# Attention products in odd slots, between the two projections, instead of at the head of even slots

## The chip, the cores and the metric

The kernel runs on one core of one Trainium2 chip. Time is device time in microseconds, the median of several executions; less is better. The program issues instructions to five engines: TensorE (PE, matmuls, with its weight loads shown as PEld), VectorE (DVE), ScalarE (ACT), GpSimd (POOL) and SyncE (SP, which issues transfers). Each engine works through its own queue in the order in which the program put the instructions there, and waits at an instruction until what it depends on is done.

## The reference

Thresholded attention, followed by a two-layer block with a hard-swish in between. Shapes: 8 batches, 8 heads, sequence 576, head size 64; then 4608 tokens, model width 512, inner width 2048.

```
scores = scale * matmul(q, k^T)                       # scale = 1/sqrt(64)
thresh = max(scores, axis=-1) - tau
scores = where(scores >= thresh, scores, -1e9)
attn   = exp(scores - max(scores)); attn /= sum(attn) + 1e-9
x      = matmul(attn, v), heads side by side          # 4608 x 512
h      = x @ w_in                                     # first projection
g      = h * clip(h + 3, 0, 6) / 6
out    = g @ w_out                                    # second projection
```

## The kernel before, in words

**Slots.** The attention of a batch is cut into 18 slots; a slot is one tile of 128 query rows for two heads (576 scores each). Eight batches make 144 slots, held in `queue`. Nothing is scheduled automatically: the order in which the Python code runs is the order in each engine's queue. Slots 0 to 13 run in a loop of their own, two at a time; slots 14 to 143 run one by one in the second loop, and what is left over runs after it.

**Score burst.** At the end of an even slot n, `burst(n + 2)` (L219) writes the scores of slots n+2 and n+3 on TensorE, the even one's last part ahead of the odd one's last part.

**Banks.** PSUM, the memory that matmuls write, is one tile `ps` of 8 banks with 512 columns each. `score_col` gives the place of the scores. An even slot has columns 896 to 1471 and 2432 to 3007 (banks 1 and 2, and banks 4 and 5); an odd slot has 64 to 639 and 1600 to 2175 (banks 0 and 1, and banks 3 and 4). First projections use bank 6 (`HB`), in some slots 7 or 0; second projections use bank 7 (`OB`). The attention products use the first 256 columns of a bank that `bank` hands out: bank 6 up to slot 13, then banks 2 and 5 in turn, and after the loop 2, 5, 0, 3 in turn.

**Max, mask, exp.** `sm_max` (L233) is a pass on VectorE for each head that copies the scores out of PSUM and takes their maximum. In slot n it is called for slot n+1, at the slot's head. GpSimd makes a bias of it (L242), ScalarE masks (L247) and takes the exponential (L252), VectorE a reciprocal (L255), GpSimd the normalised probabilities `pn` (L260), and a DMA transposes them into `pT` or, for the remaining 64 rows of each head, `pR` (L271).

**Products.** `multiply(n)` issues what the table `products` holds for slot n: `av_main` or `av_rest`, each ten groups of matmuls of probabilities and v (L289), and gives back copies out of PSUM into `xT` or `xR` on VectorE (L297, L306). The last product of a chunk of 256 rows also appends its eight first-projection items to the list `todo1`.

**Projections.** At a slot's head one item is taken from `todo1`, before `multiply` runs. `mm1` is the first projection (matmuls in L312), `mm1_relu` runs on ScalarE in odd slots (L330) and on VectorE in even slots (L332), `mm1_gate` on VectorE (L345). When the last item of a chunk has run, its pieces of the second projection go to the list `todo2`. `second` takes two of them in odd slots from 21 (`N2`) on (matmuls in L312 as well); a finished tile of four pieces is copied out by VectorE in the next even slot (`mm2_out`, L364) and written by SP.

**Other work.** Even slots hold transposes of q and k on VectorE (L96, L110); q, k and v are loaded by transfers that GpSimd's queue issues, at the end of a slot.

**Order in a slot of the second loop** (from slot 21): max of slot n+1, reciprocal of n-1, item taken, products and their copies, first projection, relu, gate, copy-out of a finished tile, second projection (odd slots), exponentials, masks, transposes, normalising, burst (even slots), output writes, loads.

Of the kernel before, what the change touches and what calls it, by code (L numbers as in the profile page):

```python
# [20 lines left out]
def kernel(  # L21
# [41 lines left out]
    ps = ps_pool.tile([P, 8, 512], F32, name="ps")  # L63
# [12 lines left out]
    def at(when, n, job):  # L76
        when.setdefault(n, []).append(job)
# [75 lines left out]
    def warm_up(count):  # L153
        for _ in range(count):
            nc.tensor.transpose(ps[:, OB, P:2 * P], identf[:], identf[:])
# [12 lines left out]
    now = -1  # L168
    turn = 0

    def bank():
        nonlocal turn
        turn += 1
        if now < N1:
            return ps[:, HB, 0:256]
        return ps[:, (2, 5)[turn % 2] if now < len(queue) else (2, 5, 0, 3)[turn % 4], 0:256]

    class Slot:
        pass
# [3 lines left out]
    queue = []  # L183
# [41 lines left out]
    def sm_max(sl):  # L225
        sl.s = s_pool.tile([P, 2, S], F32, tag="s", name="s")
        sl.m = stat_pool.tile([P, 2], F32, tag="m", name="m")
        sl.bias = stat_pool.tile([P, 2], F32, tag="bias", name="bias")
        sl.rsum = stat_pool.tile([P, 2], F32, tag="rsum", name="rsum")
        sl.rinv = stat_pool.tile([P, 2], F32, tag="rinv", name="rinv")  # L230
        for i in range(2):
            c0 = score_col(sl.n, i)
            nc.vector.tensor_scalar(out=sl.s[:, i, :], in0=ps_flat[:, c0:c0 + S],  # L233
                                    scalar1=1.0, scalar2=None, op0=Alu.mult, op1=Alu.max,
                                    accum_out=sl.m[:, i:i + 1])
            if sl.n < 3:
                sm_bias(sl, slice(i, i + 1))
        if sl.n >= 3:
            sm_bias(sl)
# [5 lines left out]
    def sm_mask(sl, i):  # L245
        s = sl.s[:, i, :]
        nc.scalar.activation(out=s, in_=s, func=Act.Prelu, bias=sl.bias[:, i:i + 1], scale=scale,  # L247
                             alpha=REJECT)

    def sm_exp(sl, i):  # L250
        s = sl.s[:, i, :]
        nc.scalar.activation(out=s, in_=s, func=Act.Exp, accum_out=sl.rsum[:, i:i + 1])  # L252

    def sm_recip(sl):
        nc.vector.reciprocal(out=sl.rinv[:], in_=sl.rsum[:])  # L255
# [36 lines left out]
    def av_main(b, hp, chunk):  # L292
        if hp == chunk == 0:
            xT[b] = x_pool.tile([P, KI, 512], BF16, tag="xT", name="xT")
        pb = bank()
        av(pb, b, hp, pts[b, hp, chunk], slice(0, 256))
        return lambda: nc.vector.tensor_copy(out=xT[b][:, hp, 256 * chunk:256 * chunk + 256], in_=pb)  # L297

    def av_rest(b):
        pb = bank()  # L300
        for hp in range(NPAIR):
            av(pb[:, 64 * hp:64 * hp + 64], b, hp, ptr[b, hp % 2], slice(64 * (hp // 2), 64 * (hp // 2) + 64))
        if b % 2 == 0:
            xR[b // 2] = x_pool.tile([P, KI, P], BF16, tag="xR", name="xR")
        o0 = 64 * (b % 2)
        return lambda: nc.vector.tensor_copy(out=xR[b // 2][:, :, o0:o0 + 64],  # L306
                                             in_=pb.rearrange("p (a b) -> p a b", a=NPAIR))
# [6 lines left out]
    def mm1(item, hb=HB):  # L314
        b, ni, c0 = item
        if c0 is None:
            for ki in range(KI):
                half_columns(ps[:, hb, :], xR[b // 2][:, ki, :], w_in_sb[:, ki, ni * P:ni * P + 512],
                             start=(ki == 0), stop=(ki == KI - 1))
        else:  # L320
            for n in range(2):
                for ki in range(KI):
                    half_columns(ps[:, hb, n * 256:(n + 1) * 256], w_in_sb[:, ki, (ni + n) * P:(ni + n + 1) * P],
                                 xT[b][:, ki, c0:c0 + 256], start=(ki == 0), stop=(ki == KI - 1))
        return ps[:, hb, :]

    def mm1_relu(hps, on_act):
        r = r_pool.tile([P, 512], F32, tag="r", name="r")[:]
        if on_act:
            nc.scalar.activation(out=r, in_=hps, func=Act.Relu, bias=three[:])  # L330
        else:
            nc.vector.tensor_scalar(out=r, in0=hps, scalar1=3.0, scalar2=0.0, op0=Alu.add, op1=Alu.max)  # L332
        return r

    def mm1_gate(item, hps, r):
        b, ni, c0 = item
        if c0 is None:
            if ni % 8 == 0:
                odd[0] = go_pool.tile([P, 1024], BF16, name="go")
            out = odd[0][:, ni % 8 * P:ni % 8 * P + 512]  # L340
        else:
            c0 += (b % 2) * (S + 64)
            out = gbuf[:, ni:ni + 2, c0:c0 + 256]
            r, hps = (x.rearrange("p (n w) -> p n w", n=2) for x in (r, hps))
        nc.vector.scalar_tensor_tensor(out=out, in0=r, scalar=6.0, in1=hps, op0=Alu.min, op1=Alu.mult)  # L345
        if c0 is None and ni % 8 == 4:
            nc.sync.dma_start_transpose(out=gbuf[:, ni - 4:ni + 4, 512:512 + P], in_=odd[0][:])
# [33 lines left out]
    def whole(b, chunk):  # L381
        mt = 5 * (b % 2) + 2 * chunk
        items = [((b, ni, 256 * chunk), ()) for ni in range(0, NI, 2)]
        items[-1] = (items[-1][0], [(b // 2, mt + i, part) for i in range(2) for part in range(4)])
        return items

    def odd_items(b, halves):
        items = [((b, ni, None), ()) for half in halves for ni in (8 * half, 8 * half + 4)]
        if 1 in halves:
            items[-1] = (items[-1][0], [(b // 2, 4, part) for part in range(4)])  # L390
        return items

    products = {}
    for b in range(B):
        n0 = b * NSLOT
        for hp in range(NPAIR):
            at(products, n0 + (6 if b == 0 else 8) + 2 * hp, (b, hp, 0))
            at(products, n0 + 18 + 2 * hp, (b, hp, 1))
        at(products, n0 + (14 if b == 0 else 16), (b, None, None))

    def multiply(n):
        copies = []
        for b, hp, chunk in products.get(n, ()):
            if hp is None:
                copies.append(av_rest(b))
                if b % 2:
                    todo1.extend(odd_items(b, (0,) if b < B - 1 else (0, 1)))
                elif b:
                    todo1.extend(odd_items(b - 1, (1,)))
            else:  # L410
                copies.append(av_main(b, hp, chunk))
                if hp == NPAIR - 1:
                    todo1.extend(whole(b, chunk))
        return copies


    for quad in range(2, 2 * B):
        b, g = divmod(quad, 2)
        n0 = (b - 1) * NSLOT
# [56 lines left out]
    for n in range(0, N1, 2):  # L476
        now = n
# [50 lines left out]
    for n, sl in enumerate(queue[N1:], N1):  # L528
        now = n
        last = queue[n - 1:n]  # L530
        if maxima < n + 1 < len(queue):
            sm_max(queue[n + 1])
            maxima = n + 1
        for prev in last:
            sm_recip(prev)
        for copy in waiting:
            copy()
        waiting = []
        item = todo1.pop(0) if todo1 else None
        for copy in multiply(n):  # L540
            copy()
        if n < N2:
            for i in range(2):
                sm_exp(sl, i)
        if item:
            item, then = item
            h = mm1(item, 0 if n == len(queue) - 1 else OB if n % 2 == 0 and not pieces else HB)
            todo2.extend(then)
            if n < N2 and n % 2:
                sm_max(queue[n + 2])  # L550
                maxima = n + 2
                warm_up(4)
            mm1_gate(item, h, mm1_relu(h, on_act=n % 2 == 1))
        for tile in outs:
            late.extend(mm2_out(*tile, on_act=False))
        outs = []
        second()
        if n >= N2:
            for i in range(2):
                sm_exp(sl, i)  # L560
        if n + 1 < len(queue):
            for i in range(2):
                sm_mask(queue[n + 1], i)
        if part == 3:
            outs.append((bb, mt))
            part = 0
        for job in jobs.get(n, ()):
            job()
        for prev in last:
            sm_norm(prev)  # L570
        if n % 2 == 0 and n + 2 < len(queue):
            burst(n + 2)
        flush(2)
        for issue in issues.get(n, ()):
            issue()
# [44 lines left out]
    now = len(queue)  # L620
# [42 lines left out]
```

## Time and profile before

| what | value |
|---|---|
| median of 3 runs | 499.06 us (499.03 to 499.36) |
| profiled execution | 499.35 us, span 497.6 us |
| granted TensorE clock | 1.00 |
| VectorE, max passes (L233) | 288, 750 ns each |
| products (L289), matmuls of 128x256 | 640, 273 ns each |
| TensorE waiting for the max, ahead of scores (L219) | 4.1 us in 16 places |
| TensorE waiting for the max, ahead of products (L289) | 2.0 us in 4 places |
| VectorE, max waiting for scores | 12.7 us in 23 places |
| probabilities' transposes (L271), issue to landing | 4.2 us median, 9.0 at most |

The span is the time from the first to the last instruction of the profiled execution, and the device time adds something to it. "Busy" is the time in which an engine had an instruction in work; matmuls overlap, so the mean duration of one is longer than its share of the time, and where times are added up, starts are used. In a timeline a row gives start, duration, engine, line, operation, output and inputs with their shape, and how many were merged; in brackets is the idle time of the engine just before, and what ended it.

### The profile page before, as it was taken

The numbers are of one execution on the slowest core, as the hardware profiler recorded it, in microseconds if no ns is written. First come the engines' busy times: TensorE is split into PE (matmuls) and PEld (weight loads), VectorE is DVE, ScalarE is ACT, GpSimd is POOL, SyncE is SP. The second block draws the span as 40 slices with busy tenths as digits, with TensorE's granted clock in tenths as the row PEclk, the third lists the DMA queues.
The fourth block names the chain that finished last, engine by engine and source line by source line (L and its number), as shares of the span: only waits on it lengthen the run. The fifth ranks groups of instructions, "written<-read, shape, count | busy, mean of one in ns | idle before, by whom it ended". The sixth has DMA issues, their size and how long they took to land.

```text
span 497.6 us, 17398 instructions
## 1 busy us (share of the span) xinstructions
PE 484.7 (97%) x6807; PEld 359.7 (72%) x6807; DVE 445.9 (90%) x1154; ACT 441.5 (89%) x949; POOL 294.4 (59%) x537
## 2 busy tenths in 40 slices
PE   8998999999999999999999999999999999999996
PEld 7766766777677776777777776777777776777474
DVE  6999998999999999999999999999999998887243
ACT  2999999999999999999999999999999999999231
POOL 3877786666666666666666666666666565555000
PEclk9999999999999999999999999999999999999999
DMA  7999899998999889998989898998999779867421
GB/s 213 166 203 200 140 166 187 220 124 157 178 171 198 119 177 183 223 139 171 175 193 179 140 166 173 204 168 147 183 182 206 130 127 133 137 117 138 89 65 42
DMA packets 192626, 79.98 MB, mean 161 GB/s; under 512 B 171168, under 2 KB 183840, under 8 KB 192544
## 3 DMA queue, kind: packets, MB, share of 16 engines
q1 hardware_dynamic: 175312, 55.34, 62.7%
q0 software_dynamic: 16896, 23.07, 24.3%
q8 instruction: 53, 0.87, 0.7%
q10 hardware_dynamic: 336, 0.46, 0.3%
q14 instruction: 29, 0.24, 0.1%
HBM read 36.70 MB, written 9.44 MB: 93 GB/s over the span
## 4 chain that ended last, share of the span: by engine, by line
PE 79%; DVE 5%; DMA 2%; issue 2%; POOL 1%; ACT 0%; SPq 0%; POOLq 0%; DVEq 0%
PE ps L312 47%; PE ps L219 25%; PE ps L289 7%; DVE s L233 3%; DMA pT<-pn 2%; POOL pn L260 1%; DVE g L345 1%; ACT r L330 0%; DVE osb L364 0%; DMA out_dram<-osb 0%; DVE r L332 0%; DVE pR L282 0%; SPq L379 0%; POOL v L119 0%; DVE xT L297 0%
## 5 line engine op out<-in xcount | busy, mean ns | idle before, releaser
L260 POOL TENSOR_SCALAR pn<-s,rinv 128x576 bf16<-128x576 f32 x288 | 211.6, 748 | 16.0 <-DVE rinv L255 1.6
L233 DVE TENSOR_SCALAR_CACHE_REDUCE s<-ps 128x576 f32<-128x576 f32 x288 | 205.0, 750 | 16.6 <-PE ps L219 12.7
L247 ACT ACTIVATE s<-s,bias 128x576 f32<-128x576 f32 x288 | 205.7, 762 | 8.8 <-POOL bias L242 8.7
L252 ACT ACTIVATE s<-s 128x576 f32<-128x576 f32 x288 | 192.3, 671 | 0.0
L219 PE MATMUL ps<-kT,qT 32*128 32x128 f32 (+3 forms) x2560 | 167.7, 414 | 4.3 <-DVE s L233 4.1
L219 PEld LDWEIGHTS ps<-kT,qT 32*128 32x128 f32 (+1 forms) x2560 | 124.5, 174 | 48.5 <-DVE s L233 11.0
L312 PE MATMUL ps<-xT,w_in_sb 128*64 128x256 bf16 (+1 forms) x1936 | 133.0, 274 | 0.5 <-DVE xT L297 0.5
L312 PE MATMUL ps<-w_out_sb,g 128*64 128x512 bf16 (+1 forms) x1024 | 131.2, 379 | 0.0
L312 PEld LDWEIGHTS <-w_in_sb 128*64 128x64 bf16 (+1 forms) x1936 | 105.7, 109 | 10.6 <-issue 3.1
L242 POOL TENSOR_SCALAR bias<-m 128x2 f32<-128x2 f32 (+1 forms) x147 | 27.8, 189 | 136.9 <-DVE rinv L255 123.4
L345 DVE SCALAR_TENSOR_TENSOR g<-r,ps 128x512 bf16<-128x512 f32 x128 | 87.3, 684 | 12.0 <-ACT r L330 8.0
L312 PEld LDWEIGHTS <-g 128*64 128x64 bf16 (+1 forms) x1024 | 61.6, 109 | 47.9 <-issue 0.2
L330 ACT ACTIVATE r<-ps,three 128x512 f32<-128x512 f32 x81 | 55.2, 686 | 19.9 <-PE ps L312 19.0
L252 ACT ACTIVATION_READ_ACCUMULATOR s<-s 128x1 f32 x288 | 54.6, 189 | 0.0
L289 PEld LDWEIGHTS <-v 128*64 128x64 bf16 x960 | 41.4, 111 | 16.0 <-issue 4.1
L289 PE MATMUL ps<-pT,v 128*64 128x256 bf16 x640 | 45.4, 273 | 1.6 <-DVE s L233 1.5
L332 DVE TENSOR_SCALAR r<-ps 128x512 f32<-128x512 f32 x63 | 43.3, 688 | 0.7 <-PE ps L312 0.4
L119 POOL DMA_DIRECT2D v<-in_v_dram x64 | 36.9, 578 | 9.3 <-DVE kT L110 5.4
L364 DVE TENSOR_SCALAR osb<-ps 128x512 f32<-128x512 f32 x32 | 21.9, 683 | 9.0 <-DMA out_dram<-osb 6.3
L110 DVE STREAM_TRANSPOSE kT<-nk 128x320 f32<-128x320 f32 (+1 forms) x64 | 26.3, 451 | 1.4 <-DMA nk<-in_k_dram 1.4
L297 DVE CAST xT<-ps 128x256 bf16<-128x256 f32 x64 | 26.0, 406 | 0.4
L96 DVE STREAM_TRANSPOSE qT<-nq 128x640 f32<-128x640 f32 (+2 forms) x33 | 24.5, 747 | 0.0
(35 smaller groups left out, 173.3 us busy)
## 6 DMA issues: line engine op xcount, KB each, us to landing
out_dram<-osb SPq DMA_DIRECT2D x140, 64.0 KB, 2.4
nk<-in_k_dram POOLq DMA_DIRECT2D x12, 576.0 KB, 4.9
nq<-in_q_dram POOLq DMA_DIRECT2D x12, 576.0 KB, 4.9
v<-in_v_dram POOLq DMA_DIRECT2D x32, 80.0 KB, 4.3
v<-in_v_dram POOLq DMA_DIRECT2D x32, 64.0 KB, 3.2
w_in_sb<-in_moe_w_in_dram POOLq DMA_DIRECT2D x4, 512.0 KB, 6.7
w_out_sb<-in_moe_w_out_dram POOLq DMA_DIRECT2D x4, 512.0 KB, 7.5
pT<-pn SPq DMA_TRANSPOSE x120, 4.2
```

The lines of the kernel that those rows point to most:

```text
L119: nc.gpsimd.dma_start(out=vsb[b % 2][32 * g:32 * g + 32].rearrange("p (hp a) c -> p a hp c", a=2)[:, a, :, c0 * D:(c0 + count) * D], in_=v ...
L219: mm = nc.tensor.matmul(ps_flat[rows, c0:c0 + w], qT[c:c + 32, j, q0:q0 + rows.stop - rows.start], kT[c:c + 32, j, k0:k0 + w], start=(j == ...
L233: nc.vector.tensor_scalar(out=sl.s[:, i, :], in0=ps_flat[:, c0:c0 + S], scalar1=1.0, scalar2=None, op0=Alu.mult, op1=Alu.max, accum_out=sl ...
L242: nc.gpsimd.tensor_scalar(out=sl.bias[:, of], in0=sl.m[:, of], scalar1=-scale, scalar2=tau, op0=Alu.mult, op1=Alu.add)
L247: nc.scalar.activation(out=s, in_=s, func=Act.Prelu, bias=sl.bias[:, i:i + 1], scale=scale, alpha=REJECT)
L252: nc.scalar.activation(out=s, in_=s, func=Act.Exp, accum_out=sl.rsum[:, i:i + 1])
L260: nc.gpsimd.tensor_scalar(out=pn[:, i, :], in0=sl.s[:, i, :], scalar1=sl.rinv[:, i:i + 1], scalar2=1.0, op0=Alu.mult, op1=Alu.mult)
L289: nc.tensor.matmul(pb[a * 64:(a + 1) * 64, :], vsb[b % 2][:, 2 * hp + a, u * D:(u + 1) * D], pT[:, block, cols], start=(c == 0), stop=(c = ...
L312: nc.tensor.matmul(out[c:c + w], lhsT[:, c:c + w], rhs, start=start, stop=stop)
L330: nc.scalar.activation(out=r, in_=hps, func=Act.Relu, bias=three[:])
L332: nc.vector.tensor_scalar(out=r, in0=hps, scalar1=3.0, scalar2=0.0, op0=Alu.add, op1=Alu.max)
L345: nc.vector.scalar_tensor_tensor(out=out, in0=r, scalar=6.0, in1=hps, op0=Alu.min, op1=Alu.mult)
```

## The change

The table `products` names another slot for each product: 7, 9, 11 and 13 of a batch for the first chunk (8 to 14 before), 15 for the remaining rows (16 before), and 17 to 23 for the second chunk (18 to 24 before). Only batch 0's first chunk (6 to 12) and remaining rows (14) stay. The main loop calls `multiply` at the old place in even slots alone; in odd slots it is called after the first projection's gate, ahead of the copy-out and the second projection. `bank` gives bank 5 in odd slots and bank 2 in even slots. As items are appended in the slot of a chunk's last product, they are appended one slot sooner too.

```diff
         if now < N1:
             return ps[:, HB, 0:256]
-        return ps[:, (2, 5)[turn % 2] if now < len(queue) else (2, 5, 0, 3)[turn % 4], 0:256]
+        return ps[:, (2, 5)[now % 2] if now < len(queue) else (2, 5, 0, 3)[turn % 4], 0:256]
...
         for hp in range(NPAIR):
-            at(products, n0 + (6 if b == 0 else 8) + 2 * hp, (b, hp, 0))
-            at(products, n0 + 18 + 2 * hp, (b, hp, 1))
-        at(products, n0 + (14 if b == 0 else 16), (b, None, None))
+            at(products, n0 + (6 if b == 0 else 7) + 2 * hp, (b, hp, 0))
+            at(products, n0 + 17 + 2 * hp, (b, hp, 1))
+        at(products, n0 + (14 if b == 0 else 15), (b, None, None))
...
         item = todo1.pop(0) if todo1 else None
-        for copy in multiply(n):
-            copy()
+        if n % 2 == 0:
+            for copy in multiply(n):
+                copy()
         if n < N2:
...
             mm1_gate(item, h, mm1_relu(h, on_act=n % 2 == 1))
+        if n % 2:
+            for copy in multiply(n):
+                copy()
         for tile in outs:
             late.extend(mm2_out(*tile, on_act=False))
```

## The prediction

> **What bounds the kernel now.** I read the busy totals and the chain of waits first, then the timeline of one steady pair of slots (an odd slot and the even one after it), then the one place where the old program already does what the new one will do everywhere.
>
> ```profile
> PE 484.7 (97%) x6807; PEld 359.7 (72%) x6807; DVE 445.9 (90%) x1154; ACT 441.5 (89%) x949; POOL 294.4 (59%) x537
> ...
> PE 79%; DVE 5%; DMA 2%; issue 2%; POOL 1%; ACT 0%; SPq 0%; POOLq 0%; DVEq 0%
> ```
>
> TensorE is busy 97% of the span and carries 79% of the chain that ended last; VectorE is close behind with 90%. So what counts is whether TensorE stays fed, and VectorE has some 10% to give. The timeline of slots 73 to 75, cut to TensorE and the VectorE rows that matter (start, duration, engine, line, operation):
>
> ```profile
> 232.60 1.06 PE L312 MATMUL ps<-xT,w_in_sb 128*64 128x256 bf16 x16
> ...
> 232.85 0.76 DVE L233 TENSOR_SCALAR_CACHE_REDUCE s<-ps 128x576 f32<-128x576 f32 x1
> ...
> 233.50 1.89 PE L312 MATMUL ps<-w_out_sb,g 128*64 128x512 bf16 x16
> ...
> 234.21 0.08 DVE L233 DVE_READ_ACCUMULATOR s<-ps 128x1 f32 x1
> ...
> 235.23 0.71 PE L289 MATMUL ps<-pT,v 128*64 128x256 bf16 x10
> ...
> 235.77 1.04 PE L312 MATMUL ps<-xT,w_in_sb 128*64 128x256 bf16 x16
> ...
> 236.74 2.23 PE L219 MATMUL ps<-kT,qT 32*128 32x128 f32 x32
> ...
> 236.86 0.69 DVE L332 TENSOR_SCALAR r<-ps 128x512 f32<-128x512 f32 x1
> ...
> 237.58 0.69 DVE L345 SCALAR_TENSOR_TENSOR g<-r,ps 128x512 bf16<-128x512 f32 x1
> 238.19 0.68 DVE L364 TENSOR_SCALAR osb<-ps 128x512 f32<-128x512 f32 x1
> ...
> 238.90 1.06 PE L312 MATMUL ps<-xT,w_in_sb 128*64 128x256 bf16 x16
> 239.15 0.76 DVE L233 TENSOR_SCALAR_CACHE_REDUCE s<-ps 128x576 f32<-128x576 f32 x1 [0.29 <-PE ps L219]
> ```
>
> Call T the start of the odd slot's first projection (232.60). From the starts, TensorE spends 0.90 us on that projection, 1.73 on the second projection, 0.54 on the products, 0.97 on the even slot's first projection and 2.16 on the score burst: 6.30, which is the pitch to the next T at 238.90, without a gap. The two max passes over the even slot's scores start at T+0.25, and the 0.29 in brackets says that they wait for the burst to write those scores; the last read-out ends at 234.29, T+1.69. Today that end has cover: the products, which write into columns 0 to 255 of bank 2 or 5, come at T+2.63, behind the second projection.
>
> Where the cover is missing, the trace shows the wait. In slots 29 to 32 no second projection is ready:
>
> ```profile
> 100.20 1.06 PE L312 MATMUL ps<-xT,w_in_sb 128*64 128x256 bf16 x16
> 101.93 0.74 PE L289 MATMUL ps<-pT,v 128*64 128x256 bf16 x10 [0.67 <-DVE s L233]
> ```
> ```profile
> 93.92:106.28 12.36, 10.56 (x154) 1.00 1.15 184
> ```
>
> The products there follow the odd slot's projection directly and start at T+1.73 instead of T+0.90, 0.05 after the second max's read-out ends (101.80+0.08 in the VectorE timeline). The second fence is the table of stretches for TensorE: length, busy, granted clock (1.00), DMA share, GB/s.
>
> **The change, part by part.** *Place on TensorE.* 64 products move from an even slot's head to between the projections of the odd slot before, always into bank 5. score_col puts an even slot's second score block at columns 2432 to 3007, and bank 5 is 2560 to 3071. So every product must wait for the second max pass of the scores that the burst has just finished. The 1.06 or so that stand before it (the projection) don't cover 1.69. Products then start at T+1.69+0.05 = T+1.74, and what is queued behind them on TensorE (second projection, next first projection, next burst) all moves back: 1.74+0.54+1.73+0.97+2.16 = 7.14 per pair, 0.84 more. It isn't won back later: the next max waits for the next burst, which sits at the end of this same queue, so the loop burst, max, products, second projection, projection, burst closes at 7.14.
>
> *VectorE behind it.* The even slot's relu on VectorE needs the even projection's end: 1.74+0.54+1.73+1.04 = T+5.05, with 0.05 for the wake-up T+5.10 (now 236.86, T+4.26). From the rows: relu to gate 0.72, gate 0.61, output copy 0.61 in every second pair, then the transposes of q or k (L96, L110) that eight of nine even slots hold, 0.70 to 0.96, about 0.8. Without an output copy VectorE is free at 5.10+0.72+0.61+0.8 = 7.23, before the next scores at 7.14+0.25 = 7.39: hidden. With it, 7.84, so the next max is 0.45 late and so is the next product. Per two pairs that is 0.45 x 8/9 = 0.40, or 0.20 per pair. Sum 1.04 per pair.
>
> *How many pairs.* From slot 33 (T=106.28) to slot 141 (T=446.94) there are 54 pairs in 340.66 us, 6.31 each. New pitch 6.30+1.04 = 7.34, +1.03 each: +55.6. One pair (slots 47 and 48) will have no second projection, some 0.7 less: +55.
>
> *Slots 14 to 32.* Slot 17's product waits for a read-out at 59.94 instead of starting at 59.73, slot 19's already waits at 65.87: +0.3. From T=69.98 to 106.28 six pairs take 36.30. Pair 21 (slots 21 and 22): +0.5 (the even slot has no product or projection left, and the burst meets the odd max instead). Pair 23: no projection ahead of the product, so T+1.74 is all idle up to it, and slot 24 gets a projection item that it lacked: 1.74+0.54+1.73+0.97+2.16 = 7.14 against 5.27, +1.9. Pairs 25 and 27: +0.84 and +1.2. Pair 29 keeps having no second projection: +0.2. Pair 31 gains one (its todo list is filled one slot earlier): 7.2 against 6.08, +1.1. Together about +6.
>
> *Tail.* One projection item (4.40 us for five, 0.88) and two pieces of the second projection (12.18 for fourteen, 0.87 each) are done in the loop instead: -2.6. One product goes into slot 143, after whose predecessor no more scores are written: nothing either way. Slot 141's own wait +0.8. Net -1.8.
>
> *What costs nothing.* Transposed probabilities are needed a slot earlier: the closest is four slots after their issue, 12.6 us, against 4.2 median and 9.0 at most from issue to landing. The v pieces: last issue in slot 4 of a batch, first product in slot 7, over two slots (6.3 us) against 4.3 to landing; if that cover went, 7 times a microsecond or two. The copy out of the product's bank moves behind the odd slot's gate; it waits for the product's end (T+2.45, against the gate's end at T+2.43), 0.02. The SP queue gets its output writes two slots earlier, still between the same transposes. ScalarE has 6.0 us of work in a pitch that grows.
>
> Sum: 55+6+0.3-1.8 = +59.5. The profiled execution's span is 497.6, so its new span is 557.1; the median 499.06 stands 1.5 above that span, so 558.6.
>
> On the clock, the nearest row is the stretch above: 85% busy with gaps of 0.17 to 0.67 us and a granted clock of 1.00; the new pitch, 6.30 busy of 7.34, is 86%. By that row the clock adds nothing. A rule speaks against this change: the Trainium skill, "TensorE: Matmul & The Clock Gate", section "A second HAM failure mode: psum-queue depth-cycling", says that short idles between groups of matmuls, from cycling through PSUM, can make the clock swing between half and full. By it alone, an estimate from that page: a pair at half clock would take 12.6 us of TensorE time, some 340 us more over 54 pairs. The trace shows no such swing with gaps of this kind, and I go by the trace.
>
> **The rivals.**
> 1. *Only the TensorE loop counts* (VectorE's lateness is absorbed): 54 x 0.83 = 44.8, less 0.7, early slots 5.3, tail -1.8: +47.6, 546.7. For it: VectorE has 10% idle now. Against: its row of work after the relu adds to 7.84. This is the low end of the forecast's own range.
> 2. *VectorE is late in every pair*: 54 x (0.84+0.45) = 69.7, early 7, tail -1.5: +75, 574. For it: transposes and reads in PSUM could run longer. Against: pairs without output copy have 0.16 to spare. The high end.
> 3. *Half hidden*: products wait only the 0.36 that bank 2's row at 95.35 shows, 62 x 0.36 = 22, plus early 3, tail -2.6: about 521. Against: bank 5 is the later one of the two, and that max had started late.
> 4. *Faster*: the product's wait is covered, and only the tail's -2.6 remains: 496.5. It needs the second max to end by T+0.90, 0.79 earlier than the rows have it, with products that write nothing the max reads; it decides where the scores of a burst would be read before its last matmuls run. Nothing shows that.
> 5. *Order not changed*: then 499; but the instruction order of the changed program has the ten product matmuls between the projections, with a wait on VectorE at the first.
>
> **How the numbers follow.** The forecast, +47 to +75 around 558.6 with rivals 1 and 2 as its ends, has 0.82; rival 3 and what lies between it and 546 has 0.10; more than 574, 0.04; faster 0.02; no change 0.02. The measurement can tell about 0.2% (1 us). The range 545 to 573 leaves out less than 2 in 10. Faster 0.02, same 0.02, slower 0.96.
>
> **What would show it.** Waits of L289 on VectorE's max go from 2.0 us in 4 to 45 to 65 us in about 60; products start at T+1.74, never before the second read-out; T to T alternates between about 7.1 and 7.6; the wait of max for the burst goes where an output copy precedes it; the clock stays at 1.00; from the last T to the end is some 2 us shorter. The prediction is wrong if products start ahead of the read-out, or if the pitch stays near 6.3.

## The result, and the profile after

The changed kernel takes 556.62 us (median of 6 runs, 556.54 to 557.21) against 499.2 us for the kernel before on the same chip: 1.115 times as long, interval 1.114 to 1.117, or 57.4 us more. The profiled execution's span went from 497.6 to 554.8 us. The forecast was 558.6.

From the page of the changed kernel, the totals, the chain that ended last, and the group of the products (busy, mean ns of one, then idle time just ahead of it and what ended it):

```profile
PE 493.3 (89%) x6823; PEld 375.5 (68%) x6823; DVE 455.7 (82%) x1156; ACT 440.8 (79%) x947; POOL 294.6 (53%) x537
...
PE 59%; DVE 27%; issue 4%; DMA 0%; SPq 0%; DVEq 0%
...
L289 PE MATMUL ps<-pT,v 128*64 128x256 bf16 x640 | 47.5, 274 | 44.7 <-DVE s L233 44.6
```

The work is the same but for 16 matmuls (what is done in the loop rather than behind it is issued in halves), and every engine's share has fallen. TensorE's part of the chain went from 79 to 59%, and VectorE's rose from 5 to 27%. The table of waits gives it by pair of lines (total, times, longest), first of the kernel before, then of the changed one:

```profile
PE ps L289 <- DVE s L233: 2.0, 4, 0.7
```
```profile
PE ps L289 <- DVE s L233: 50.0, 62, 1.7
```

One steady stretch of the changed kernel's timeline, TensorE and VectorE, two pairs of slots with T at 249.80 and 256.97:

```profile
249.80 1.06 PE L312 MATMUL ps<-xT,w_in_sb 128*64 128x256 bf16 x16
250.05 0.76 DVE L233 TENSOR_SCALAR_CACHE_REDUCE s<-ps 128x576 f32<-128x576 f32 x1 [0.27 <-PE ps L219]
...
251.41 0.08 DVE L233 DVE_READ_ACCUMULATOR s<-ps 128x1 f32 x1
...
251.55 0.74 PE L289 MATMUL ps<-pT,v 128*64 128x256 bf16 x10 [0.68 <-DVE s L233]
...
252.09 1.92 PE L312 MATMUL ps<-w_out_sb,g 128*64 128x512 bf16 x16
...
253.82 1.07 PE L312 MATMUL ps<-xT,w_in_sb 128*64 128x256 bf16 x16
...
254.81 2.23 PE L219 MATMUL ps<-kT,qT 32*128 32x128 f32 x32
...
254.92 0.69 DVE L332 TENSOR_SCALAR r<-ps 128x512 f32<-128x512 f32 x1 [0.75 <-PE ps L312]
...
256.25 0.68 DVE L364 TENSOR_SCALAR osb<-ps 128x512 f32<-128x512 f32 x1
...
256.85 0.83 DVE L96 STREAM_TRANSPOSE qT<-nq 128x640 f32<-128x640 f32 x1
256.97 1.06 PE L312 MATMUL ps<-xT,w_in_sb 128*64 128x256 bf16 x16
257.61 0.72 DVE L233 TENSOR_SCALAR_CACHE_REDUCE s<-ps 128x576 f32<-128x576 f32 x1
...
259.07 0.74 PE L289 MATMUL ps<-pT,v 128*64 128x256 bf16 x10 [1.04 <-DVE s L233]
...
264.50 1.06 PE L312 MATMUL ps<-xT,w_in_sb 128*64 128x256 bf16 x16
```

The products start at T+1.75, 0.06 after the second read-out ends (251.49). The pair is 7.17 long. VectorE then waits 0.75 for the even slot's projection, copies out a tile, transposes q, and starts the next max at 0.64 past the next T instead of 0.25; the products of that pair come at 259.07, T+2.10, and the pair is 7.53 long.

By stretches (length, then busy time of the engines, clock), first of the kernel before, then of the changed one: slots 33 to 141.

```profile
106.28:446.94 340.66, 339.63 (x5123) 252.46 (x5120) 327.33 (x845) 324.72 (x703) 214.20 (x389) 1.00 0.92 165
```
```profile
111.81:505.71 393.90, 350.05 (x5124) 267.89 (x5120) 335.57 (x846) 324.44 (x702) 214.62 (x389) 1.00 0.81 143
```

That is 53.2 us of the 57.2 that the span grew by. Slots 21 to 32 went from 36.30 to 42.53 (+6.2), and from slot 141 to the end from 50.62 to 49.09 (-1.5). The changed kernel reached slot 21 0.7 earlier. Of this, 0.56 is there already in the first max pass of all (8.78, 9.34 before), where the two programs are still the same. Over the eleven traces of this case that pass starts between 8.78 and 9.34, so these 0.56 are a spread of the start and not an effect of the change.

### The profile page after: what moved, and what is told of

It reads as the page before. It is cut to its first block, busy times and chain, and to the rows that moved or that the text cites. A ratio compares the mean times of both kernels' runs of the same rounds, so it can differ in the third digit from the quotient of the medians.

```text
span 554.8 us, 17429 instructions
## 1 busy us (share of the span) xinstructions
PE 493.3 (89%) x6823; PEld 375.5 (68%) x6823; DVE 455.7 (82%) x1156; ACT 440.8 (79%) x947; POOL 294.6 (53%) x537
## 4 chain that ended last, share of the span: by engine, by line
PE 59%; DVE 27%; issue 4%; DMA 0%; SPq 0%; DVEq 0%
PE ps L312 34%; DVE s L233 18%; PE ps L219 17%; PE ps L289 9%; DVE r L332 3%; DVE osb L364 2%; DVE kT L110 1%; DVE g L345 1%; DVE qT L96 1%; DVE xT L297 0%; DMA out_dram<-osb 0%; DVE pR L282 0%; SPq L379 0%; DVEq L364 0%; DVE go L345 0%
## 5 line engine op out<-in xcount | busy, mean ns | idle before, releaser
L219 PE MATMUL ps<-kT,qT 32*128 32x128 f32 (+3 forms) x2560 | 165.9, 414 | 4.3 <-DVE s L233 3.4
L312 PE MATMUL ps<-xT,w_in_sb 128*64 128x256 bf16 (+1 forms) x1944 | 134.8, 274 | 1.2 <-DVE xT L297 1.2
L312 PE MATMUL ps<-w_out_sb,g 128*64 128x512 bf16 (+1 forms) x1032 | 133.3, 379 | 0.0
L312 PEld LDWEIGHTS <-w_in_sb 128*64 128x64 bf16 (+1 forms) x1944 | 110.0, 109 | 18.3 <-issue 3.8
L312 PEld LDWEIGHTS <-g 128*64 128x64 bf16 (+1 forms) x1032 | 74.7, 109 | 34.8 <-issue 0.4
L289 PE MATMUL ps<-pT,v 128*64 128x256 bf16 x640 | 47.5, 274 | 44.7 <-DVE s L233 44.6
L289 PEld LDWEIGHTS <-v 128*64 128x64 bf16 x960 | 42.6, 110 | 63.7 <-issue 62.9
L332 DVE TENSOR_SCALAR r<-ps 128x512 f32<-128x512 f32 x64 | 44.1, 689 | 43.7 <-PE ps L312 43.7
L119 POOL DMA_DIRECT2D v<-in_v_dram x64 | 36.8, 575 | 33.8 <-PE ps L219 25.8
```

The source lines that it names most:

```text
L119: nc.gpsimd.dma_start(out=vsb[b % 2][32 * g:32 * g + 32].rearrange("p (hp a) c -> p a hp c", a=2)[:, a, :, c0 * D:(c0 + count) * D], in_=v ...
L219: mm = nc.tensor.matmul(ps_flat[rows, c0:c0 + w], qT[c:c + 32, j, q0:q0 + rows.stop - rows.start], kT[c:c + 32, j, k0:k0 + w], start=(j == ...
L289: nc.tensor.matmul(pb[a * 64:(a + 1) * 64, :], vsb[b % 2][:, 2 * hp + a, u * D:(u + 1) * D], pT[:, block, cols], start=(c == 0), stop=(c = ...
L312: nc.tensor.matmul(out[c:c + w], lhsT[:, c:c + w], rhs, start=start, stop=stop)
```

## The experiments

Pitches below are from T to T. The mean is over the 54 pairs from slot 33 to slot 141 (changed kernel 7.29, kernel before 6.31).

### The wait taken away: the second max pass reads another bank

```diff
-            c0 = score_col(sl.n, i)
+            c0 = score_col(sl.n + (i == 1 and sl.n > N1 and sl.n % 2 == 0), i)
```

> The changed kernel, with one thing left out: from slot 15 on, an even slot's second max pass reads the odd slot's second block (columns 1600 to 2175) in place of its own, so nothing reads bank 5 and those probabilities are of other scores. VectorE does the same work, the products stay between the projections. Theory (the wait on bank 5 is the whole loss): products at T+0.90, pitch 6.30 to 6.4, 496 to 502. Rival (the place between the projections costs by itself, through VectorE's order or TensorE's weight loads): 520 or more.

504.31 us, 1.0105 of the kernel before (1.009 to 1.012). With the place between the projections kept and only the wait gone, 52 of the 57 us are gone. The timeline of this kernel, one pair, TensorE and one row of GpSimd:

```profile
261.41 1.06 PE L312 MATMUL ps<-xT,w_in_sb 128*64 128x256 bf16 x16
262.31 0.71 PE L289 MATMUL ps<-pT,v 128*64 128x256 bf16 x10
262.85 1.89 PE L312 MATMUL ps<-w_out_sb,g 128*64 128x512 bf16 x16
264.58 1.04 PE L312 MATMUL ps<-xT,w_in_sb 128*64 128x256 bf16 x16
265.55 2.34 PE L219 MATMUL ps<-kT,qT 32*128 32x128 f32 x32
...
265.99 1.47 POOL L260 TENSOR_SCALAR pn<-s,rinv 128x576 bf16<-128x576 f32 x2
...
267.82 1.06 PE L312 MATMUL ps<-xT,w_in_sb 128*64 128x256 bf16 x16
```

The products start at T+0.90 without a wait. But the pitch is 6.41, over the theory's 6.30, and the time is 2.3 over the expected range: the burst takes 2.27 (265.55 to 267.82) where it took 2.16. Its last four matmuls wait for a relay in GpSimd's queue (the `nop` in `burst`), which stands there behind the normalising. The next run asks whether the relay comes late.

### The same, with the products' copies at the next slot's head

Beside the edit above, against the changed kernel:

```diff
         if n % 2:
-            for copy in multiply(n):
-                copy()
+            waiting = multiply(n)
...
+    for copy in waiting:
+        copy()
```

> The kernel whose even slots' second max pass reads the odd slot's second block (so nothing reads bank 5), and whose products' copies stand at the next slot's head, behind the odd slot's max. It asks why that kernel's pitch was 6.41 and not 6.30. Theory (the copy ahead of the odd max made the reciprocal, GpSimd's normalising and the relay behind it late for the burst's last matmuls): pairs without the end of a chunk take 6.30, pairs with one take 0.4 to 0.9 more, since the next item waits for the copy, 15 to 16 of them: 503 to 512 in all. Rival (the products' place between the projections costs 0.11 by itself): 6.41 in pairs without the end of a chunk.

509.81 us. Pairs without a chunk's end fell from 6.41 to 6.30, pairs with one take 7.10 to 7.40. So the place between the projections costs nothing by itself. The copy ahead of the odd max had put the reciprocal 0.34 later (T+4.12 against T+3.78), and the relay came 0.10 and the burst's last four matmuls 0.11 later (T+6.09 against T+5.98 for the first of them): the 0.11 per pair. In the changed kernel this is covered: there GpSimd waits for the burst (25.8 us in 44 places), not the burst for GpSimd.

### Which bank, or which pass: bank 2, and the passes swapped

```diff
-        return ps[:, (2, 5)[now % 2] if now < len(queue) else (2, 5, 0, 3)[turn % 4], 0:256]
+        return ps[:, 2 if now < len(queue) else (2, 5, 0, 3)[turn % 4], 0:256]
```

> The changed kernel with bank 2 in place of bank 5 in all slots of the loop; bank 2 is read by the first max pass alone, whose read-out ends at T+1.02. Theory (wait for the pass that reads the bank): products at T+1.07, TensorE's loop 1.07+0.54+1.73+0.97+2.16 = 6.47, VectorE late by 0.45 in pairs with an output copy, 0.20 in the mean, as with bank 5: 6.67 per pair, 6.67-7.29 = -0.62 over 54 pairs, -34, and some -3 in slots 21 to 32: about 520 (513 to 526). Rival (the loss is in the place, not in the bank): 550 or more.

```diff
-        for i in range(2):
+        for i in ((0, 1) if sl.n % 2 or sl.n <= N1 else (1, 0)):
             c0 = score_col(sl.n, i)
```

> The changed kernel, bank 5 as it has it, with the two max passes of an even slot in the other order, so that bank 5 is read first. Theory (what counts is which pass reads the bank): as with bank 2, products at T+1.07, 512 to 522. Rival (bank 5 is worse than bank 2 for another reason): 545 or more.

517.01 us and 517.65 us; mean pitches 6.62 and 6.64. Two different edits that both make the products wait for the first pass instead of the second give nearly the same time, so it is the pass, not the bank. The second of them, one pair in its timeline, a pair where VectorE is on time:

```profile
234.81 1.06 PE L312 MATMUL ps<-xT,w_in_sb 128*64 128x256 bf16 x16
235.90 0.74 PE L289 MATMUL ps<-pT,v 128*64 128x256 bf16 x10
236.44 1.92 PE L312 MATMUL ps<-w_out_sb,g 128*64 128x512 bf16 x16
238.17 1.07 PE L312 MATMUL ps<-xT,w_in_sb 128*64 128x256 bf16 x16
239.17 2.23 PE L219 MATMUL ps<-kT,qT 32*128 32x128 f32 x32
241.33 0.85 PE L312 MATMUL ps<-xT,w_in_sb 128*64 128x256 bf16 x12
```

The products start at T+1.09, 0.19 later than T+0.90, and no wait is shown at all. The reason is in how the profile models a matmul's end: the projection's last matmul is drawn to T+1.06. So a stall on TensorE is read from starts, and the table of waits gives too little.

### More of the same wait: products at the odd slot's head

```diff
-        if n % 2 == 0:
-            for copy in multiply(n):
-                copy()
+        for copy in multiply(n):
+            copy()
...
-        if n % 2:
-            for copy in multiply(n):
-                copy()
```

> The changed kernel with the products at the odd slot's head, ahead of the first projection (copies at the old place): the wait for the second read-out at T+1.69 then has no cover at all, and the first projection is queued behind it too. Theory: TensorE's loop 1.74+0.54+0.90+1.73+0.97+2.16 = 8.04, with VectorE's part 8.2 to 8.5 per pair, +0.9 to +1.2 on 7.29, over 54 pairs +49 to +65, and some 5 in slots 21 to 32: 605 to 627. Rival (what counts is that products stand between the two projections): under 540.

630.74 us, 1.263 of the kernel before. With no cover at all the pitch is 8.35 to 8.6. The time is 3.7 above the range. The profiled execution, the longest of its four (633.16), shows where: ahead of slot 21, where the expectation counted nothing, it is 4.4 behind the changed kernel, and slots 21 to 32 cost 10.8 where 5 were expected, while the 54 pairs cost 62, within the range. In two stretches the pairs took up to 9.9, and there matmuls ran slower. From its timeline and its table of stretches (length, busy, clock):

```profile
89.49 1.45 PE L289 MATMUL ps<-pT,v 128*64 128x256 bf16 x10 [1.99 <-DVE s L233]
...
99.39 0.74 PE L289 MATMUL ps<-pT,v 128*64 128x256 bf16 x10 [1.67 <-DVE s L233]
```
```profile
73.69:135.50 61.81, 47.47 (x644) 39.69 (x644) 42.71 (x111) 41.37 (x90) 27.40 (x50) 0.92 0.60 115
```

The first row's ten groups take 1.45 us where they take 0.74 elsewhere, after a gap of 1.99 us. The granted clock is 0.92 over that stretch, and 1.00 in most others.

### VectorE's share: finished tiles copied out by ScalarE

```diff
         for tile in outs:
-            late.extend(mm2_out(*tile, on_act=False))
+            late.extend(mm2_out(*tile, on_act=True))
```

> The changed kernel with the finished tiles of the main loop copied out by ScalarE in place of VectorE. Theory (pairs with an output copy are longer because VectorE comes late to the next max): every pair falls to TensorE's 7.17; the changed kernel's 54 pairs take 393.9, and 53 x 7.17 + 6.49 (the pair without a second projection) is 386.5, so -7.4: 549 (546 to 552), with no difference between even and odd pairs. Rival (the transposes or the copies of the products make those pairs long): 555 to 558.

550.05 us, 6.6 less than the changed kernel. Its timeline:

```profile
225.74 1.06 PE L312 MATMUL ps<-xT,w_in_sb 128*64 128x256 bf16 x16
...
232.91 1.06 PE L312 MATMUL ps<-xT,w_in_sb 128*64 128x256 bf16 x16
...
240.09 1.06 PE L312 MATMUL ps<-xT,w_in_sb 128*64 128x256 bf16 x16
```

The pairs of 7.5 are gone: 7.17, 7.18, and a mean of 7.18. So the copy-out was what made VectorE late, and the rest, 0.87 per pair, is the loop through the max. A dozen pairs of 7.26 to 7.40 are left; six of them are longer in the kernel before too (6.39), and the other six are not explained here.

### All of the change but the place: products behind the second projection

```diff
-        if n % 2:
-            for copy in multiply(n):
-                copy()
...
         second()
+        if n % 2:
+            waiting = multiply(n)
...
+    for copy in waiting:
+        copy()
```

> All of the change but the place: the products of the odd slot stand behind its second projection, and their copies at the head of the next slot, as before the change; they are issued, and their items appended, one slot sooner. Theory (the wait for the second max pass is the whole loss): the products start at T+2.63, past the read-out at T+1.69, the pitch is 6.30 again. The tail loses one projection item and two pieces (-2.6), slots 24 and 31 take them (+0.97 and some 0.3 to 1.1): 497.5 to 499.5. Rival (being a slot sooner costs by itself: transposes or v not there, bank 5 alone): 510 or more, with waits of the products on DMAs.

509.65 us, 1.0212 of the kernel before (1.0197 to 1.0227). The wait for the max is gone and most pairs take 6.30, but this is 10 us over the theory's range, just under the rival's 510, and the rival's waits on DMAs are not there either. What the table of waits shows instead, and one place of it in the timeline (TensorE, then VectorE's copy):

```profile
PE ps L312 <- DVE xT L297: 11.5, 15, 1.2
```
```profile
136.15 0.71 PE L289 MATMUL ps<-pT,v 128*64 128x256 bf16 x10
136.70 0.49 PE L312 MATMUL ps<-xT,w_in_sb 128*64 128x256 bf16 x6
137.84 0.74 PE L312 MATMUL ps<-xT,w_in_sb 128*64 128x256 bf16 x10 [0.65 <-DVE xT L297]
```
```profile
137.39 0.40 DVE L297 CAST xT<-ps 128x256 bf16<-128x256 f32 x1
```

Items are now appended in an odd slot, so the even slot's projection right behind a chunk's last product already reads that product's copy, and the copy sits behind the odd slot's max on VectorE. The seventh matmul waits. That happens 15 times, for 0.8 to 1.1 in pitch each. The changed kernel doesn't have this: there the second projection lies between that product and that item.

### Both waits avoided: a chunk's last product between the two pieces

Against the run before, the main lines:

```diff
...
+            if chunk_end(now) and part % 2 == 0:
+                for copy in multiply(now):
+                    copy()
...
-        if n % 2:
+        if n % 2 and not (pieces and chunk_end(n)):
             waiting = multiply(n)
```

`chunk_end` is true in odd slots that hold a chunk's last product, which goes into bank 2; the other products of the loop take banks 2 and 5 in turn again.

> Products one slot sooner, behind the odd slot's second projection with their copies at the next slot's head, but the last product of a chunk between the two pieces of the second projection, in bank 2, with its copy at once. It asks whether the sooner start can be had without the two waits. That product starts at T+0.90+0.87 = T+1.77, past bank 2's read-out at T+1.02 (or T+1.4 where VectorE is late); its copy is done near T+2.9, before the next projection's seventh matmul at T+3.5 needs it. Theory: the 15 pairs with a chunk's end fall from 7.1 to 7.4 to 6.3 to 6.6 (the copy ahead of the odd max still delays the reciprocal by 0.34): 509.65 - 15 x 0.7 = 499, 497.5 to 501. Rival (the chunk's end costs by something else than the copy): 505 or more.

500.65 us, 1.0031 of the kernel before (1.0019 to 1.0044). One chunk's end in its timeline:

```profile
132.06 1.05 PE L312 MATMUL ps<-w_in_sb,xR 128*64 128x512 bf16 x8
132.95 1.03 PE L312 MATMUL ps<-w_out_sb,g 128*64 128x512 bf16 x8
133.81 0.71 PE L289 MATMUL ps<-pT,v 128*64 128x256 bf16 x10
134.36 1.03 PE L312 MATMUL ps<-w_out_sb,g 128*64 128x512 bf16 x8
135.22 1.04 PE L312 MATMUL ps<-xT,w_in_sb 128*64 128x256 bf16 x16
136.19 2.42 PE L219 MATMUL ps<-kT,qT 32*64 32x128 f32 x64
138.54 1.06 PE L312 MATMUL ps<-xT,w_in_sb 128*64 128x256 bf16 x16
```

No gap before the product at T+1.75, none before or in the next projection; what is left at a chunk's end is the burst's 2.35, 2.18 in the kernel before (the pair is 6.48). So 9 of the 10.6 us that the run before lost were the copy. From slot 141 to the end this kernel is 2.4 shorter than the kernel before (48.25 against 50.62), and the loop gives it back: +0.9 in slots 21 to 32 and +2.9 in the 54 pairs, most of it at the chunks' ends. The sooner start by itself gains nothing.

### Two slots sooner, at the head of even slots

```diff
-            at(products, n0 + (6 if b == 0 else 8) + 2 * hp, (b, hp, 0))
-            at(products, n0 + 18 + 2 * hp, (b, hp, 1))
-        at(products, n0 + (14 if b == 0 else 16), (b, None, None))
+            at(products, n0 + 6 + 2 * hp, (b, hp, 0))
+            at(products, n0 + 16 + 2 * hp, (b, hp, 1))
+        at(products, n0 + 14, (b, None, None))
...
-        v_pieces(b, (13, 14, 15, 16, 17, 18, 19, 20) if b == 1 else [(b - 1) * NSLOT + n for n in range(8, 24, 2)])
+        v_pieces(b, (13, 14, 15, 16, 17, 18, 19, 20) if b == 1 else [(b - 1) * NSLOT + n for n in range(6, 22, 2)])
```

> The kernel before, products two slots sooner and still at the head of even slots (from batch 1 on 6 to 12, 14, 16 to 22; batch 0's second chunk 16 to 22), the v pieces issued two slots sooner too. Items are appended two slots sooner, and a chunk's copy again has the rest of an even slot before the first item that reads it. From the kernel before: the tail loses two items (1.76) and two pieces (1.74), slots 23 and 24 go from 5.27 to 6.30, slots 31 and 32 from 6.08 to 6.30: -2.2, 496 to 498. Rival (the loop has no room for it, or probabilities and v are not there yet): 499 or more, with waits of the products.

516.64 us, 1.0366 of the kernel before. The rival was right: the products now wait for the transposed probabilities. Its waits, its worst place and the stretch around it:

```profile
PE ps L289 <- DMA pT<-pn: 11.6, 13, 4.9
```
```profile
71.99 1.28 PE L289 MATMUL ps<-pT,v 128*64 128x256 bf16 x10 [4.95 <-DMA pT<-pn]
```
```profile
60.00:80.00 20.00, 14.96 (x178) 11.23 (x176) 13.26 (x36) 11.62 (x24) 9.50 (x18) 0.83 0.76 131
```

At one slot sooner none of the runs shows this wait on a matmul of the products (a weight load waits 0.3 and 0.4 us once in two of them); at two slots the cover is used up, and around the longest gap the clock falls as well. No version that was run beats the kernel before.

## Why the prediction was right

*The wait on bank 5.* Right in place and size: products forecast at T+1.74, found at T+1.75 where VectorE is on time; 45 to 65 us in about 60 places, found 50.0 in 62. That it is the cause is shown by taking the bank out of the max's way (52 of 57 us gone), by cutting the wait from 0.84 to 0.2 in two ways (517 and 518) and by taking the cover away (631).

*The loop closes at 7.14.* Found 7.17 where VectorE is on time; the run with ScalarE's copy-out has a mean of 7.18.

*VectorE late behind the copy-out.* The mechanism was right: relu at T+5.12 (5.10), next max at T+7.81 (7.84). The size was nearly twice what it should be: 0.20 per pair was forecast, and the run without it saved 6.1 us in the 54 pairs, 0.11 each. That is the term that was mis-sized. Pair by pair against that run, 20 pairs are longer, by 0.22 to 0.42 and 0.30 in the mean; the forecast had 24 (eight of nine in 27) by 0.45. Seven of the 27 pairs with a copy-out have no transposes behind it, not three: in the last batch nothing is left to transpose. Part of the size is that transposes were counted by their durations, 0.8; the one above has 0.83 in its row and takes 0.76 from start to start (256.85 to 257.61).

*The sum.* 54 pairs +53.2 (forecast +55), slots 21 to 32 +6.2 (+6), tail -1.5 (-1.8). Up to slot 21 it was -0.7 instead of +0.3: 0.56 is the earlier start, and the two pairs from slot 17 are each 0.07 shorter although slot 17's product does wait, 0.20. The 54 pairs came nearer than their parts, and that is luck: VectorE's lateness was 4.7 under its forecast (6.1 against 10.8) and the loop 3.0 over (47.1 against 44.1), and the two nearly cancel.

*What costs nothing.* Right for the changed kernel: no product waited for a transpose or for v. Two of these covers were tested away. The transposes' cover holds one slot and not two. The copy's cover is the second projection itself, which the forecast had not seen as a cover: it named the copy's 0.02 on VectorE, and not that the next projection reads it. Those 0.02 were too small as well: in the changed kernel the copies wait for their products 4.7 us in 22 places, at no cost in the pairs shown, as VectorE then waits 0.75 for the even slot's projection anyway.

*The clock.* By the row at 85% busy nothing was counted; the changed kernel's mean is 0.999. The swing that the Trainium skill describes ("TensorE: Matmul & The Clock Gate", "A second HAM failure mode: psum-queue depth-cycling") did not come with gaps of 0.7 to 1.1 us in every pair. In the run with gaps of 1.7 to 2.0 us the clock fell to 0.92 and 0.91 in two stretches (61.8 and 20 us long) and stayed at 1.00 in the others.

*The rivals.* "Half hidden" and "faster" fell: the products waited for the second pass in 62 places. "VectorE is late in every pair" fell too: 20 of the 54 are late. The end with the TensorE loop alone (546.7) lies 3.4 under the run that has only that loop (550.05); 1.6 of it is 7.17 in place of 7.14 in 54 pairs.

## What to carry to other kernels

Before a matmul group is moved, ask who last read the bank that it writes and when that read ends, counted from the same mark as the new start; a read that waits for the end of TensorE's own queue turns the wait into a loop, which later slack can't win back. Look also for what the moved work's old neighbours were covering for others: here the second projection covered the max pass for the products, and then the copy of the products for the next projection. Where both covers are wanted, splitting the covering group gave both here (500.65 us), though no gain over the kernel before.

## What the runs showed of the hardware that was not expected

A gap on TensorE of 1.99 us was followed by matmuls that took twice as long (1.45 against 0.74 us for the ten groups), while gaps of 1.67 to 1.91 us mostly left the clock at 1.00; the granted clock was 0.92 over the 61.8 us around it. That run has two more such spells. One, with a clock of 0.50 from 115 to 120 us, begins within a score burst and not behind a gap of this kind; the other follows a gap of 1.91 us at 464.25, while gaps of 1.91 us at 312.42, 346.19 and 499.41 left the clock at 1.00. So the length of the last gap does not decide it alone, and what does stays open. And the profile's idle time ahead of a matmul is too short by some 0.17 us per wait, since the end of the matmul before it is drawn later than the next one could start: with bank 2 the table of waits shows 8.0 us for the products in 23 places, while slots 33 to 141 alone took 17.0 us more than before (357.7 against 340.66), part of it VectorE's lateness.
